# Four edits to the first stages of an attention and two-MLP kernel: where the decay factors are loaded, which banks the first transposes use, where the second group is normalised, and how far the second products lag

## The chip, the cores and the metric

The kernel runs on one core of one Trainium2 chip, as one program in one launch. The metric is the device time of one execution in microseconds; the median of several runs counts.

## The reference

The reference chains three computations. The first is a linear recurrence with a complex decay, for 4 batches, 8 heads, 768 steps and head size 48:

```python
scale = np.minimum(mag, 0.999) / (mag + 1e-06)         # mag = |a_re + i a_im|
for t in range(S):
    S_re, S_im = ar*S_re - ai*S_im + kv, ar*S_im + ai*S_re   # kv: outer product of k and v
    y[:, :, t] = einsum('bhd,bhde->bhe', q[:, :, t], S_re)
```

Its output, as 3072 tokens of 384 columns, goes through `silu(x @ w_gate) * (x @ w_val) @ w_out` with 1536 inner columns, and that through `h = x @ w_in; (h - tanh(h)) @ w2_out` with 2048 inner columns. The MLP weights are float64 arrays, all else is float32.

## The kernel before, in words

**Units and groups.** The recurrence is computed in 24 units of 128 steps (6 for each batch). Two units make a group. For each group, `group_steps` normalises the decays (`squares`, `norm_root`, `norm`), transposes them on PE (`put_a`: three transposes into one PSUM bank, then copies by ACT into the tile PL), forms running products of the complex decays in 14 dependent steps on DVE (`cstep`, L278 to L281), copies them into NW, works out a few small per-group factors (`lam`) and a reciprocal (W[2], L357 to L365). The factors are stored to DRAM (L351) and read back in another layout as the tile LS (L355, four loads of 3 KB). The first group is normalised before its transposes; the second inside the first group's `cstep` loop (L316 to L321); later ones inside the loop of the group ahead of them (L304).

For each unit, `unit_a` transposes q and k, scales them into QK (L390), stores QK to DRAM (L392) and reads it back as TK and TQ (L397). `unit_b` multiplies TK by TQ into scores (psS, L434), masks them, updates the running state (Hn, from Z and LS, on POOL, L427 to L429) and forms the output y, which goes by DMA into x, the input of the first MLP.

**MLP tiles.** `moe1_tile` runs the first MLP over 8 tiles of 2, 2, 2, 3, 3, 4, 4 and 4 units. Each has 12 steps f: 18 matmuls of the first layer (L581), silu on ACT (L585), a product and a split into a high and a low half (t, hi, lo; L590, L540, L541), and 9 matmuls of the second layer (L565), which wait in a list, `pend`, and are issued by `catch_up(lag)`. The lag is one step. Attention work for the next tile is traced between the matmuls (`bg`), and in the first tile also the decoding of the float64 weights (`dec1`, `decode`): DMA of the raw words, ACT L144, DVE L145 to L148, ACT L154, and then either two PE passes and ACT L164 or DVE L156. The weight of the second layer has two buffers (wo).

**Order.** Each engine runs its own list in order. The lists are drawn up when the program is built: a scheduler of the framework simulates time, and each engine takes, among the instructions whose inputs and buffers are ready at that simulated moment, the one that was traced first. `issue_after` holds a set of instructions behind a named one: the weights of the first tile (L719) are decoded after the last `cstep` of the first group. All DMAs are issued from one queue, SP's.

**PSUM.** There are eight banks: two named at, one psA (used by `put_a`), two l1 and three l2. Until the first MLP tile begins, `PA` hands out the two at and three l2 banks in turn (L130).

Of the kernel before, what the change touches and what calls it, by code (L numbers as in the profile page):

```python
# [8 lines left out]
F32 = mybir.dt.float32  # L9
F32R = mybir.dt.float32r  # L10
# [7 lines left out]
P = 128  # L18
# [23 lines left out]
def tile_kernel(ctx: ExitStack, tc: tile.TileContext, q, k, v, a_re, a_im, w_gate, w_val, w_out, w2_in, w2_out, out):  # L42
# [18 lines left out]

    N_PRE, QAT, QDEP = 8, 15, 4
    SHARE0, SHARE1, SHARE, RATE = 1, 0, 2.0, 6
    NORM_AT, NA0, SCM = 5, 1, 8

    N_A, N0, W2STEP, LON = 8, 20, 2, 10
    TU = max(TILES)
# [195 lines left out]

    def put_a(u, g, pl, PL, A0):
        t = st["a"][pl][:, g]
        ps = ps_g.tile([P, 512], F32, tag="psA", name="psA")
        for j in range(NJ):
            PE.transpose(ps[:, P * j:P * (j + 1)], t[:, P * j:P * (j + 1)], ident)
        p = ps[:, 0:DM].rearrange("p (j t) -> p j t", j=NJ)
        for h, x in ((1, p[:, :, HALF:P]), (0, p[:, :, HALF:0:-1])):  # L270
            ACT.copy(out=PL[:, :, pl, :, g, :, h].rearrange("p e b j -> p j b e"), in_=x.rearrange("p j (b e) -> p j b e", e=8))
        ACT.copy(out=A0[:, pl, :, g], in_=p[:, :, 0])
# [10 lines left out]
    def group_steps(g0):  # L283
        grp = list(range(g0, g0 + G))

        PL = pl_p.tile([P, 8, 2, 8, G, NJ, 2], F32, tag="PL", name="PL")
        A0 = a1.tile([P, 2, NJ, G], F32, tag="A0", name="A0")
        if g0 == 0:
            squares(DVE)
            norm_root(0)  # L290
            norm(DVE)
            yield
        for g, u in enumerate(grp):
            for pl in (1, 0):
                put_a(u, g, pl, PL, A0)
                yield
        load_a(g0 + G)
        for c in range(2):
            DVE.memset(PL[:, 0, c, 0, :, :, 0], 1.0 - c)
        flat = PL.rearrange("p e c b g j h -> p e c (b g j h)")  # L300
        for e in range(1, 8):
            cstep(flat[:, e - 1], flat[:, e], 1)
            yield
            if e == NORM_AT and 0 < g0 < NU - G:  # L304
                squares(POOL)
                norm_root(g0 + G)
                yield
                norm(POOL)
                yield
        rows = PL.rearrange("p e c b g j h -> p (e c) b (g j h)")  # L310
        for b in range(1, 8):
            cs = cstep(rows[:, 14:16, b - 1], rows[:, :, b], 8)
            if g0 == 0:
                prog["cs"] = cs.ins
            yield
            if g0 == 0 and b == NA0:  # L316
                squares(DVE)
                norm_root(G)
                yield
                norm(DVE)  # L320
                yield  # L321

        NW = a1.tile([P, 3, G, NJ, P], F32, tag="NW", name="NW", bufs=1)
        for c in range(2):
            nw = NW[:, c].rearrange("p g j (h b e) -> p h (g j) b e", h=2, e=8)
            ACT.copy(out=nw[:, 1], in_=PL[:, :, c, :, :, :, 1].rearrange("p e b g j -> p (g j) b e"))
            ACT.copy(out=nw[:, 0], in_=PL[:, ::-1, c, ::-1, :, :, 0].rearrange("p e b g j -> p (g j) b e"))
        yield

        sh = [P, 2, NJ, G]  # L330
        T0, pr = T("T0", sh), T("lp", [P, 2, 2, NJ, G])
        for i in range(2):
            DVE.tensor_tensor(out=pr[:, i], in0=PL[:, 7, :, 7, :, :, 0].rearrange("p c g j -> p c j g"), in1=A0[:, i].unsqueeze(1).to_broadcast(sh), op=ALU.mult)
        DVE.tensor_tensor(out=T0[:, 0], in0=pr[:, 0, 0], in1=pr[:, 1, 1], op=ALU.subtract)
        DVE.tensor_tensor(out=T0[:, 1], in0=pr[:, 1, 0], in1=pr[:, 0, 1], op=ALU.add)
        WL = a2.tile([P, 2, NJ, G + 1], F32, tag="wl", name="WL")
        DVE.tensor_copy(out=WL[:, :, :, 1:G + 1], in_=PL[:, 7, :, 7, :, :, 1].rearrange("p c g j -> p c j g"))
        if g0 > 0:
            DVE.tensor_copy(out=WL[:, :, :, 0], in_=st["wl"][:, :, :, G])
        else:  # L340
            DVE.memset(WL[:, :, :, 0], 1.0)
        st["wl"] = WL
        pr2 = T("lp", [P, 2, 2, NJ, G])
        for i in range(2):
            DVE.tensor_tensor(out=pr2[:, i], in0=T0, in1=WL[:, i, :, 0:G].unsqueeze(1).to_broadcast(sh), op=ALU.mult)
        L = a1.tile([P, NJ, 3, G], F32, tag="lam", name="lam")
        DVE.tensor_tensor(out=L[:, :, 0, :], in0=pr2[:, 0, 0], in1=pr2[:, 1, 1], op=ALU.add)
        DVE.tensor_tensor(out=L[:, :, 1, :], in0=pr2[:, 1, 0], in1=pr2[:, 0, 1], op=ALU.subtract)
        DVE.tensor_tensor(out=L[:, :, 2, :], in0=pr2[:, 0, 1], in1=pr2[:, 1, 0], op=ALU.subtract)
        lam_g = lam_d[g0 // G]  # L350
        SP.dma_start(out=lam_g.rearrange("(j p) c g -> p j c g", p=P), in_=L)  # L351
        LS = a2.tile([D2, H, 2, G], F32, tag="ls", name="LS")
        for i in range(2):
            for c in range(2):
                SP.dma_start(out=LS[i * D:(i + 1) * D, :, c, :], in_=lam_g[:, c * (1 + i), :].rearrange("(h d) g -> d h g", h=H))  # L355
        yield
        W = [NW[:, c].rearrange("p g j t -> p (g j t)") for c in range(3)]  # L357
        x1, x2 = W[2], T("x2")
        ACT.activation(out=x1, in_=W[0], func=AF.Square)
        ACT.activation(out=x2, in_=W[1], func=AF.Square)  # L360
        DVE.scalar_tensor_tensor(out=x1, in0=x1, scalar=-1.0, in1=x2, op0=ALU.mult, op1=ALU.subtract)
        ACT.activation(out=x2, in_=x1, func=AF.Abs_reciprocal_sqrt, scale=-1.0, bias=tiny)
        ACT.activation(out=x2, in_=x2, func=AF.Square, accum_out=chk[:, 1, g0 // G:g0 // G + 1])
        DVE.tensor_tensor(out=x1, in0=x1, in1=x2, op=ALU.mult)
        DVE.scalar_tensor_tensor(out=W[2], in0=x1, scalar=2.0, in1=x2, op0=ALU.add, op1=ALU.mult)  # L365
        yield
        for g, u in enumerate(grp):
            st["w", u] = (NW, LS, g)
        yield

    def unit_a(u):


        qn, kn = st.pop(("q", u)), st.pop(("k", u))
        NW, LS, g = st["w", u]
        W = [NW[:, c, g] for c in range(3)]
        qk = a1.tile([P, 2, NJ, P], F32, tag="qk", name="qk")
        for i, x in enumerate((qn, kn)):
# [16 lines left out]
        for i, x in ((1, TK), (0, TQ)):  # L395
            for c in range(2):
                SP.dma_start(out=x[c * D:(c + 1) * D], in_=d[i, c].rearrange("(h d) t -> d h t", h=H))  # L397
        yield
        Kn = a1.tile([P, H, 2, D], F32, tag="Kn", name="Kn")
        for c in range(2):  # L400
# [142 lines left out]
    def MT(tag, bufs, dt=F32):  # L543
        return m1.tile([P, N1], dt, tag=tag, name=tag, bufs=bufs)
# [7 lines left out]
    def moe1_tile(ti, bg):  # L552
# [3 lines left out]
        tok = tile_u0[ti] * P  # L556
        acc = []

        def l2(f, m):
            if f == 0:  # L560
                acc.extend(ps_2.tile([P, 512], F32, tag="l2", name="acc")[:, 0:n_t] for _ in range(NJ))
            w = wo_t.pop(ti * NF1 + f)
            for j in range(NJ):
                for i, (a, b) in enumerate(PASSES):
                    PE.matmul(acc[j], lhsT=w[:, a, j * P:(j + 1) * P], rhs=m[b], start=(f == 0 and i == 0), stop=(f == NF1 - 1 and i == 2))  # L565
            if f == NF1 - 1:

                oh, ol = (t[:, :, 0:n_t] for t in x)
                for j in range(NJ):
                    ACT.copy(out=oh[:, j], in_=acc[j])  # L570
                    DVE.tensor_tensor(out=ol[:, j], in0=acc[j], in1=oh[:, j].bitcast(F32), op=ALU.subtract)  # L571
                for c, t in enumerate((oh, ol)):
                    SP.dma_start(out=o_d[:, c, :, tok:tok + n_t], in_=t.bitcast(F32))

        for f in range(NF1):
            ps = []
            for i, w in enumerate((wg_hl[f], wv_hl[f])):
                p = ps_1.tile([P, 512], F32, tag="l1", name="l1")[:, 0:n_t]
                for n in range(3 * NJ):
                    kk, (a, b) = n // 3, PASSES[n % 3]  # L580
                    PE.matmul(p, lhsT=w[a][:, kk], rhs=x[b][:, kk, 0:n_t], start=(n == 0), stop=(n == 3 * NJ - 1))  # L581
                ps.append(p)
                if i == 0:
                    s = MT("t", MID)[:, 0:n_t]
                    ACT.activation(out=s, in_=p, func=AF.Silu)  # L585
                    if f == 0:
                        catch_up(0)
                    bg(2 * f)
            catch_up(1)
            DVE.tensor_tensor(out=s, in0=s, in1=ps[1], op=ALU.mult)  # L590
            m = [MT(tag, MID, F32R)[:, 0:n_t] for tag in ("hi", "lo")]
            split(s, *m)
            load_wo(ti * NF1 + f)
            pend.append(lambda f=f, m=m: l2(f, m))
# [336 lines left out]
```

## Time and profile before

| what | value |
|---|---|
| median of 3 runs | 1236.8 us (1231.5 to 1237.46) |
| profiled execution, its own time | 1240.99 us |
| its span | 1239.2 us |
| PE, PEld, DVE, ACT busy | 1092.8, 972.8, 987.2, 655.7 us |
| mean granted TensorE clock | 0.943 of full speed |

The profile comes from one execution. Busy times of different engines overlap. Times of PE are modelled and overlap one another in dense stretches. The first matmul of the first MLP starts at 118.36 us, the second tile begins at about 200.5 us and the third at about 276 us.

### The profile page before, as it was taken

The numbers are of one execution on the slowest core, as the hardware profiler recorded it, in microseconds if no ns is written. First come the engines' busy times: TensorE is split into PE (matmuls) and PEld (weight loads), VectorE is DVE, ScalarE is ACT, GpSimd is POOL, SyncE is SP. The second block draws the span as 40 slices with busy tenths as digits, with TensorE's granted clock in tenths as the row PEclk, the third lists the DMA queues.
The fourth block names the chain that finished last, engine by engine and source line by source line (L and its number), as shares of the span: only waits on it lengthen the run. The fifth ranks groups of instructions, "written<-read, shape, count | busy, mean of one in ns | idle before, by whom it ended". The sixth has DMA issues, their size and how long they took to land. (4 is left out here: it accounts for less than half of the span.)

```text
span 1239.2 us, 18491 instructions
## 1 busy us (share of the span) xinstructions
PE 1092.8 (88%) x6504; PEld 972.8 (78%) x6504; DVE 987.2 (80%) x2010; ACT 655.7 (53%) x1247; POOL 125.9 (10%) x110
## 2 busy tenths in 40 slices
PE   3157857879989999889999999989999999999997
PEld 2145846878988888877878888878999999999996
DVE  4878968965979788596885338989888888888886
ACT  5446537375563754536535224565565655555553
POOL 0012321202122122021211000000000000000000
PEclk9567977998999999889999999999999999999999
DMA  6397777887886878686666658642100102020000
GB/s 152 74 214 173 159 162 191 218 187 189 207 206 145 198 195 184 146 216 151 151 165 170 169 138 282 211 158 95 51 27 25 53 1 77 1 77 1 26 1 28
DMA packets 296741, 163.37 MB, mean 132 GB/s; under 512 B 157505, under 2 KB 273857, under 8 KB 296641
## 3 DMA queue, kind: packets, MB, share of 16 engines
q1 hardware_dynamic: 296640, 162.11, 52.1%
q8 instruction: 53, 0.87, 0.3%
q14 instruction: 48, 0.39, 0.1%
HBM read 111.82 MB, written 37.86 MB: 121 GB/s over the span
## 5 line engine op out<-in xcount | busy, mean ns | idle before, releaser
L581 PE MATMUL l<-x,wgv 128*128 128x256 f32 (+2 forms) x1728 | 351.9, 351 | 12.7 <-ACT t L585 10.3
L581 PEld LDWEIGHTS l<-x,wgv 128*128 128x128 f32 x1728 | 285.6, 197 | 42.4 <-ACT t L585 13.8
L663 PE MATMUL l<-x,wi 128*128 128x512 f32 x864 | 214.0, 393 | 5.0 <-DVE t L611 5.0
L645 PE MATMUL l<-w,hi 128*128 128x384 f32 x768 | 190.2, 338 | 0.0
L663 PEld LDWEIGHTS l<-x,wi 128*128 128x128 f32 x864 | 161.1, 188 | 34.8 <-DVE t L611 6.1
L565 PE MATMUL acc<-hi,wo 128*128 128x256 f32 (+2 forms) x576 | 166.9, 350 | 8.5 <-ACT wo L154 3.4
L540 ACT CAST hi<-t 128x512 fp32r<-128x512 f32 (+2 forms) x192 | 108.6, 566 | 120.8 <-DVE t L590 89.6
L645 PEld LDWEIGHTS l<-w,hi 128*128 128x128 f32 x768 | 140.9, 189 | 7.8 <-DVE x L571 0.4
L541 DVE TENSOR_TENSOR lo<-t,hi 128x512 fp32r<-128x512 f32 (+2 forms) x192 | 124.6, 649 | 27.1 <-ACT hi L540 26.8
L604 ACT ACTIVATE t<-l 128x512 f32<-128x512 f32 x96 | 57.3, 597 | 147.1 <-PE l L663 143.0
L645 PE MATMUL l<-w,lo 128*128 128x384 f32 x384 | 122.3, 337 | 0.4 <-DVE lo L541 0.4
L565 PEld LDWEIGHTS acc<-hi,wo 128*128 128x128 f32 x576 | 105.6, 195 | 19.6 <-ACT wo L154 4.2
L278 DVE TENSOR_TENSOR prod<-PL 128x384 f32<-128x384 f32 x168 | 105.3, 627 | 2.7
L565 PE MATMUL acc<-lo,wo 128*128 128x256 f32 (+2 forms) x288 | 98.2, 345 | 0.0
L434 PE MATMUL psS<-TQ,TK 96*128 96x128 f32 x384 | 61.1, 314 | 38.1 <-DMA TQ<-qk_d 21.7
L606 DVE TENSOR_TENSOR l<-l,t 128x512 f32<-128x512 f32 x96 | 67.0, 698 | 33.5 <-ACT uu L605 33.3
L434 PEld LDWEIGHTS psS<-TQ,TK 96*128 96x128 f32 x384 | 56.8, 223 | 43.2 <-issue 24.7
L590 DVE TENSOR_TENSOR t<-t,l 128x256 f32<-128x256 f32 (+2 forms) x96 | 52.5, 547 | 33.6 <-PE l L581 20.1
L611 DVE COPY_PREDICATED t<-far,l 128x512 f32<-128x512 int32 x96 | 71.0, 739 | 2.6
L585 ACT ACTIVATE t<-l 128x256 f32<-128x256 f32 (+2 forms) x96 | 47.1, 490 | 48.3 <-PE l L581 44.2
L645 PEld LDWEIGHTS l<-w,lo 128*128 128x128 f32 x384 | 71.4, 188 | 0.8 <-DVE lo L541 0.8
L610 DVE SCALAR_TENSOR_TENSOR t<-vv,t 128x512 f32<-128x512 f32 x96 | 66.1, 689 | 6.8
(128 smaller groups left out, 1670.6 us busy)
## 6 DMA issues: line engine op xcount, KB each, us to landing
wo<-wo_d SPq DMA_DIRECT2D x84, 384.0 KB, 4.0
qk_d<-QK SPq DMA_DIRECT2D x24, 768.0 KB, 5.0
TK<-qk_d SPq DMA_DIRECT2D x48, 192.0 KB, 4.2
TQ<-qk_d SPq DMA_DIRECT2D x48, 192.0 KB, 4.9
x<-o_d SPq DMA_DIRECT2D x12, 768.0 KB, 6.0
x<-y SPq DMA_DIRECT2D x48, 144.0 KB, 4.4
raw<-in_moe_w_in_dram SPq DMA_DIRECT2D x16, 384.0 KB, 4.1
raw<-in_moe_w_out_dram SPq DMA_DIRECT2D x16, 384.0 KB, 3.2
```

Source lines behind the costliest of these rows:

```text
L278: DVE.tensor_tensor(out=pr, in0=prev.unsqueeze(2).to_broadcast(sh), in1=cur.unsqueeze(1).to_broadcast(sh), op=ALU.mult)
L434: PE.matmul(ps[:, P * i:P * (i + 1)], lhsT=TK[:, 4 * hh + i], rhs=TQ[:, 4 * hh + i], start=True, stop=True)
L540: ACT.copy(out=hi, in_=t)
L541: DVE.tensor_tensor(out=lo, in0=t, in1=hi.bitcast(F32), op=ALU.subtract)
L565: PE.matmul(acc[j], lhsT=w[:, a, j * P:(j + 1) * P], rhs=m[b], start=(f == 0 and i == 0), stop=(f == NF1 - 1 and i == 2))
L581: PE.matmul(p, lhsT=w[a][:, kk], rhs=x[b][:, kk, 0:n_t], start=(n == 0), stop=(n == 3 * NJ - 1))
L604: ACT.activation(out=t, in_=p, func=AF.Tanh)
L606: DVE.tensor_tensor(out=p, in0=p, in1=t, op=ALU.subtract)
L610: DVE.scalar_tensor_tensor(out=t, in0=vv, scalar=G_F, in1=t, op0=ALU.add, op1=ALU.mult)
L611: DVE.copy_predicated(out=t, mask=far, data=p)
L645: PE.matmul(acc[tb], lhsT=g[a][:, tb * P:(tb + 1) * P], rhs=w2_hl[f][:, b], start=(f == 0 and n == 0), stop=(f == NF2 - 1 and n == 2))
L663: PE.matmul(p, lhsT=wi_hl[a][:, kk, sl], rhs=x[b][:, kk, :], start=(n == 0), stop=(n == 3 * NJ - 1))
```

## The change

Four edits. (1) LS is no longer loaded in `group_steps` behind the store of the factors, but in `unit_a` of the first unit of a group, behind the loads of TK and TQ. (2) `put_a` of the first two units takes its bank from `PA` instead of the single bank psA. (3) The three calls that normalise the second group move from the eighth `cstep` of the first group to the end of its `group_steps`. (4) In MLP tiles 0 and 1, `catch_up` leaves four steps waiting instead of one, the list is not emptied at the start of tile 1, and t, hi and lo of two steps share one buffer of 512 columns (each step of these tiles has 256).

```diff
     def put_a(u, g, pl, PL, A0):
-        ps = ps_g.tile([P, 512], F32, tag="psA", name="psA")
+        ps = PA("psA") if u < 2 else ps_g.tile([P, 512], F32, tag="psA", name="psA")
...
-            if g0 == 0 and b == NA0:
-                squares(DVE)
-                norm_root(G)
-                yield
-                norm(DVE)
-                yield
...
-        LS = a2.tile([D2, H, 2, G], F32, tag="ls", name="LS")
-        for i in range(2):
-            for c in range(2):
-                SP.dma_start(out=LS[i * D:(i + 1) * D, :, c, :], in_=lam_g[:, c * (1 + i), :].rearrange("(h d) g -> d h g", h=H))
...
-            st["w", u] = (NW, LS, g)
+            st["w", u] = [NW, None, g]
         yield
+        if g0 == 0:
+            squares(DVE)
+            norm_root(G)
+            yield
+            norm(DVE)
+            yield
...
         for i, x in ((1, TK), (0, TQ)):
             for c in range(2):
                 SP.dma_start(out=x[c * D:(c + 1) * D], in_=d[i, c].rearrange("(h d) t -> d h t", h=H))
+        if g == 0:
+            LS = a2.tile([D2, H, 2, G], F32, tag="ls", name="LS")
+            for i in range(2):
+                for c in range(2):
+                    SP.dma_start(out=LS[i * D:(i + 1) * D, :, c, :], in_=lam_d[u // G][:, c * (1 + i), :].rearrange("(h d) g -> d h g", h=H))
+            for n in range(G):
+                st["w", u + n][1] = LS
...
+        near = ti < 2
...
-                    s = MT("t", MID)[:, 0:n_t]
+                    if not near:
+                        s = MT("t", MID)[:, 0:n_t]
+                    else:
+                        if f % 2 == 0:
+                            mid = [MT(tag, MID, dt) for tag, dt in (("t", F32), ("hi", F32R), ("lo", F32R))]
+                        s, *m = [t[:, f % 2 * (N1 // 2):][:, 0:n_t] for t in mid]
                     ACT.activation(out=s, in_=p, func=AF.Silu)
-                    if f == 0:
+                    if f == 0 and ti != 1:
                         catch_up(0)
                     bg(2 * f)
-            catch_up(1)
+            catch_up(4 if near else 1)
             DVE.tensor_tensor(out=s, in0=s, in1=ps[1], op=ALU.mult)
-            m = [MT(tag, MID, F32R)[:, 0:n_t] for tag in ("hi", "lo")]
+            if not near:
+                m = [MT(tag, MID, F32R)[:, 0:n_t] for tag in ("hi", "lo")]
```

## Rows read from the trace of the kernel before

**Rows 1.** Windows by stage: span, busy time of each engine, granted clock, DMA share, GB/s.
```profile
0.00:118.36 118.36, 52.74 (x230) 35.11 (x230) 88.82 (x195) 61.76 (x121) 13.48 (x23) 0.74 0.66 148
118.36:200.50 82.14, 58.45 (x437) 54.56 (x438) 67.43 (x145) 44.76 (x92) 22.82 (x15) 0.81 0.73 166
200.50:276.00 75.50, 62.90 (x510) 58.90 (x508) 62.29 (x153) 45.55 (x93) 12.31 (x10) 0.95 0.83 207
276.00:420.00 144.00, 129.43 (x998) 125.64 (x999) 111.15 (x257) 79.19 (x159) 29.42 (x24) 0.94 0.78 184
420.00:1239.20 819.20, 789.30 (x4334) 698.57 (x4332) 657.54 (x1264) 424.45 (x784) 47.83 (x38) 0.98 0.41 110
```
**Rows 2.** PE's waits, first two MLP tiles: waiter, ender, us in total, times, longest.
```profile
PE psA L268 <- ACT A L272: 14.3, 4, 11.7
PE l L581 <- ACT t L585: 6.7, 6, 2.0
PE psS L434 <- DMA TQ<-qk_d: 6.1, 3, 5.1
PE acc L565 <- ACT wo L154: 3.4, 3, 1.9
PE acc L565 <- DMA wo<-wo_d: 1.9, 3, 0.9
PE acc L565 <- DVE wo L156: 1.1, 2, 0.5
PE acc L565 <- ACT hi L540: 0.9, 1, 0.9
```
**Rows 3.** Timeline of ACT around the first transposes: start, duration, instruction, idle before.
```profile
25.68 0.84 ACT L271 COPY PL<-psA 128x192 f32<-128x192 f32 x2 [1.64 <-PE psA L268]
...
26.36 0.89 ACT L164 CAST wgv<-psL 128x384 fp32r<-128x384 f32 x2
...
32.22 0.21 ACT L272 COPY A<-psA 128x3 f32<-128x3 f32 x1
```
**Rows 4.** Timeline of DVE during the first group's steps.
```profile
32.58 0.56 DVE L278 TENSOR_TENSOR prod<-PL 128x384 f32<-128x384 f32 x1
...
33.64 0.56 DVE L278 TENSOR_TENSOR prod<-PL 128x384 f32<-128x384 f32 x1
...
38.79 0.95 DVE L241 TENSOR_TENSOR s<-s,s 128x768 f32<-128x768 f32 x1
...
52.76 1.02 DVE L145 TENSOR_SCALAR dt<-dt 128x768 f32<-128x768 f32 x2
53.70 0.24 DVE L333 TENSOR_TENSOR lp<-PL,A 128x12 f32<-128x12 f32 x2
```
**Rows 5.** Timeline of SP's queue around the first load of LS.
```profile
65.92 4.82 SPq L355 DMA_DIRECT2D LS<-lam_d  x4
...
71.98 0.41 SPq L392 DMA_DIRECT2D qk_d<-QK  x1
```
**Rows 6.** Timeline of DVE: the first unit's QK.
```profile
66.00 1.82 DVE L390 TENSOR_TENSOR QK<-qk,NW 128x768 f32<-128x768 f32 x2
```
**Rows 7.** PE's waits before the first MLP tile.
```profile
PE psS L434 <- DMA TQ<-qk_d: 6.9, 1, 6.9
```
**Rows 8.** DMA issues of the whole span: count, KB each, median us to landing.
```profile
TQ<-qk_d SPq DMA_DIRECT2D x48, 192.0 KB, 4.9
...
LS<-lam_d SPq DMA_DIRECT2D x48, 3.0 KB, 2.5
```
**Rows 9.** Timeline of ACT shortly before the first MLP tile.
```profile
108.60 0.87 ACT L326 COPY NW<-PL 128x384 f32<-128x384 f32 x1 [0.83 <-DVE PL L280]
109.37 0.58 ACT L468 CAST y<-psY 128x512 fp32r<-128x512 f32 x1
```
**Rows 10.** Timeline of PE in the first MLP tile.
```profile
187.16 0.90 PE L268 MATMUL psA<-ident,ar 128*128 128x128 f32 x3 [11.70 <-ACT A L272]
```
**Rows 11.** Window of 20 us around it, columns as in the first group.
```profile
180.00:200.00 20.00, 9.75 (x41) 8.66 (x42) 15.80 (x41) 16.87 (x35) 3.35 (x3) 0.50 0.62 147
```

More of the change, by code (lines that the diff above doesn't have):

```diff
@@ L63, in tile_kernel @@
     SHARE0, SHARE1, SHARE, RATE = 1, 0, 2.0, 6
-    NORM_AT, NA0, SCM = 5, 1, 8
+    NORM_AT, SCM = 5, 8
     N_A, N0, W2STEP, LON = 8, 20, 2, 10
@@ L367, in group_steps @@
         for g, u in enumerate(grp):
-            st["w", u] = (NW, LS, g)
+            st["w", u] = [NW, None, g]
         yield
+        if g0 == 0:
[4 more added lines that the diff above has]
+            yield
     def unit_a(u):
         qn, kn = st.pop(("q", u)), st.pop(("k", u))
-        NW, LS, g = st["w", u]
+        NW, _, g = st["w", u]
         W = [NW[:, c, g] for c in range(3)]
```

## The prediction

> **What bounds the kernel now.** I read the stages first, then what PE waits for in each, then the timelines around the four edits. The chain that ended last names only the last store and says nothing of the start. The stages [rows 1] show two kernels in one. From 276 us on PE is busy 129.4 of 144.0 and 789.3 of 819.2 us: PE's own work sets the time there, and nothing in the change touches that work. Before 118.36 us the first MLP has not begun, and PE has only decoding and attention to do. Between 118.36 and 276 us, in the first two MLP tiles, PE stands still for 82.14 - 58.45 = 23.7 and 75.50 - 62.90 = 12.6 us, together 36.3, and runs the first tile at a mean clock of 0.81. DVE is the busiest of the others (67.4 of 82.1, 62.3 of 75.5), and DMA is at 0.73 and 0.83. So the change can be worth two things: the moment at which the first tile starts, and part of those 36.3 us. A start that comes earlier is kept to the end, if the stage after it can follow, because PE is full from 276 us on.
>
> **The change part by part.**
>
> **Banks.** In the kernel before the four sets of transposes of units 0 and 1 share one bank, so each waits until ACT has emptied it, and ACT meanwhile takes decoding casts. ACT begins the copies at 25.68 and ends the last at 32.22 + 0.21 = 32.43 [rows 3], 6.75 us for four sets. One set holds ACT for 26.36 - 25.68 = 0.68 us, the start of its first copy to the start of what follows; four back to back take 2.7, end at about 28.5, and save 3.9. The other bound is 0, if a cast still falls between every two sets. I take 3.0: the first cast pair (0.89 us [rows 3]) still gets in once. The decoding is pushed back by as much; its cover is that the weights are first used at 118.36 us, and if that cover is gone the 3.0 go with it. Giving PA four more turns changes which bank a later tile gets, not how many there are: 0, and at most the 0.9 of one such set of transposes [rows 10] either way.
>
> **Norm of the second group.** The 14 steps run from 32.58 to 52.76, 20.2 us. Undisturbed a step takes 33.64 - 32.58 = 1.06, 14 take 14.8: the second group's norm costs the first group 5.4 us [rows 4]. Behind the group it would give 5.4 back. But the edit changes only the order of tracing, and the scheduler fills by readiness. Decoding traced far later stands right behind the last step (52.76), ahead of the group's own product L333 (53.70) [rows 4], since L333's input was not ready; and the norm's first sum runs at 38.79, behind the sixth step (32.58 + 6 x 1.06 = 38.9), though it was traced behind the eighth. As the steps depend on one another, each leaves a gap, and the norm is ready in the same gaps as before. So I take 0. Bounds: a gain of 5.4, and a loss of 5.4, if what the first group gains the second loses and the second ends last [rows 9].
>
> **LS.** The four loads hold SP's queue from 65.92 to 70.74, because the factors' store has to land first. The first unit's QK is ready at 66.00 + 1.82 = 67.82 and its store leaves at 71.98 [rows 5, 6]: 4.2 us late. Behind that store hang TK, TQ and the scores, for which PE then waits 6.9 us [rows 7]; the second unit follows on the same buffers. Moved, the loads pass an ar load, weight loads, the store and TK and TQ. I take 3.9 of the 4.2, since the ar and weight loads still stand in the queue; bounds 0 (queue held by something else) and 4.8 (all of the hold). In exchange four issues of about 0.4 us, as the store's [rows 5], now stand between TQ and the weight loads behind it: 1.6 us, covered because decoding runs ahead of its use. LS itself lands 1.6 + 2.5 = 4.1 us after TQ's issue, TQ 4.9 [rows 8], so no unit waits for it: 0. If it did, the price would be 1.6 for each of the two groups that follow in tiles 0 and 1, 3.2 together.
>
> Does the start keep 3.0 + 3.9 = 6.9? The last link before 118.36 is y of the second unit, which stands on ACT behind a copy that waits for the second group's steps on DVE [rows 9]. DVE is busy 88.8 of 118.4 us [rows 1], so it has 29.5 idle from which to make up 6.9, and the same two edits start its work earlier. I keep all of it; the lower bound is 0.
>
> **Lag.** With four steps waiting, a second product no longer stands close behind its split, its weight or its cast. What PE waited for at the products themselves is 3.4 + 1.9 + 1.1 + 0.9 = 7.3 us [rows 2], and this goes. Three things come late next. The weight has two buffers, so the weight of step f + 2 can be finished only once product f is done; product f + 2 is two steps later, as before. A buffer of hi and lo holds two steps, so in every even step ACT's cast waits for a product issued in that same step: 12 such steps; ACT is busy 44.8 of 82.1 and 45.6 of 75.5 us [rows 1] and covers it, but queued behind that cast on ACT are the silu of the next step, which frees the l1 bank for PE, and the copies that free psA. And tile 1's first product comes one step, not two, behind tile 0's last, whose three banks have to be emptied in between. For these I set 2.8 against the 7.3, an estimate by L581's own longest wait (2.0) and the one cast wait (0.9) [rows 2]. Net 4.5. Bounds: 7.3 + 6.7 = 14.0, if the waits for silu go too, and -6.7, if these double.
>
> What lies behind an engine's front can't come forward: the transposes at 187.16 waited 11.7 us [rows 10], and second products stood right behind them. The Trainium skill (PSUM — Partial Sum Buffer, Engine vs sequencer instructions) says that matmuls start and complete in program order. By that rule a product that is ready four steps early is worth only the 7.3 us of its own waits; without it, it could reach into all 36.3. The trace agrees: no matmul ran in those 11.7 us.
>
> Sum: 3.0 + 0 + 3.9 + 4.5 = 11.4 us. Within the profiled execution: 1240.99 (span 1239.2, 1.8 around it) becomes 1229.6. That execution lies 4.2 above the median of the runs, 1236.8, and I predict against the median: 1236.8 - 11.4 = 1225.4, so 1225.
>
> **The rivals.**
>
> A: the norm truly stands behind the first group, because buffers or ACT hold it back. Then 5.4 more come off the start: 1220. For it: 5.4 us stand in the rows as the norm's. Against it: the early sum and the decoding in the gaps [rows 4].
>
> B: the start is earlier, but the first two tiles give it back, and the lag only moves waits. For it: 14.3 + 6.7 + 6.1 = 27.1 us of waits there [rows 2] (psA, silu, TQ) are not removed by any edit, and DVE is at 82% in both tiles [rows 1], with the same decoding and attention to do. Against: DVE has 28 us idle there. Then 6.9 and 4.5 are both lost: 1237.
>
> C, slower: one more set of later transposes falls into the wrong place. From unit 2 on psA is still a single bank, emptied by ACT in its order, and PE's order is fixed when the program is built; every edit redraws it. One such wait cost 11.7 us [rows 10], and around it the clock was 0.50, the lower of the two levels (1.2 GHz), at which 9.75 us of PE's work [rows 11] take about 4.9 longer than at the upper: 16.6 in all. With four products behind it, it takes the lag's gain too: 1236.8 - 6.9 + 16.6 = 1246.5. It decides as soon as the new order has one more wait of over 7 us at L268 than the old. For it: psA is the largest wait of the stage [rows 2]. Against: there were four of them, only one of them long, and the redrawn order may as well lose that one.
>
> **How the numbers follow.** Forecast 0.49 (its own range 1215 to 1231), A 0.14, B 0.20, C 0.17. The range: below, A with the lag's upper bound, 1219 - 9.5 = 1210; above, C's middle part up to 1244, leaving out about one in ten on each side. Within 0.5% is 1230.6 to 1243.0, about what a measurement of this kernel can tell from no change. Faster: 0.45 of the forecast's 0.49, A's 0.14 and 0.03 of B: 0.62. Slower: 0.14 of C and 0.03 of B: 0.17. Same: the rest, 0.21.
>
> **What would show it.** Banks: the first step on DVE near 29.6 instead of 32.58. Norm: its sums still between the first group's steps, which last about 20 us; 15 would be A. LS: the store of QK within 1 us of QK's end, at about 66; the first matmul of the first MLP near 111.5. Lag: no wait of PE at L565 in the first two tiles, and the third tile beginning near 264 to 265. Wrong would be a first tile that starts at 111 and a third that still begins near 276 (B), an L268 wait of over 7 us more (C), or waits at L581 for silu well over 6.7 us.

## The result and the profile after

The changed kernel takes 1245.2 us (median of 5, 1242.66 to 1247.34) against 1236.3 us for the kernel before on the same chip (median of 5, 1231.5 to 1237.46): ratio 1.0072, interval 1.0057 to 1.0087. It is slower by about 9 us where 11 us of gain were forecast, and lies just above the forecast's range (1210 to 1244).

The two profiled executions differ by less: 1242.66 us is the fastest of the kernel after, and 1240.99 us lies above all five timed runs of the kernel before. So the traces tell where work went, and the ratios tell how much.

The stages of the kernel after, columns as in [rows 1]; the first ends where the first MLP tile begins:

```profile
0.00:104.11 104.11, 43.55 (x221) 28.39 (x221) 73.11 (x149) 54.19 (x105) 9.72 (x22) 0.80 0.74 162
104.11:200.00 95.89, 68.13 (x431) 61.62 (x432) 80.33 (x183) 45.81 (x93) 14.83 (x13) 0.77 0.61 159
200.00:280.00 80.00, 65.88 (x549) 62.34 (x548) 65.90 (x165) 53.03 (x109) 16.69 (x14) 0.92 0.81 191
280.00:420.00 140.00, 122.43 (x937) 116.49 (x936) 107.66 (x249) 76.79 (x154) 27.88 (x24) 0.94 0.76 177
420.00:1241.00 821.00, 795.05 (x4373) 704.23 (x4372) 657.77 (x1267) 427.42 (x788) 44.81 (x38) 0.99 0.41 111
```

The first tile begins 14.3 us earlier than before (104.11 against 118.36). Only 65.62 - 60.56 = 5.06 us of that are idle time of PE that is gone; the other 9.2 are work that PE has not done yet (43.55 us busy ahead of the tile, 52.74 before [rows 1]). Up to 200 us PE then stands still for 95.89 - 68.13 = 27.8 us, against 82.14 - 58.45 = 23.7 in a shorter stretch before [rows 1].

A tile has 216 matmuls of the first layer, so the start of each tile can be counted. In the kernel before the second tile begins at 205.07 and the third at 281.82; the 200.5 and 276 of the section on its profile are the ends of the first layers ahead of them. In the kernel after the first tile's end at 154.87, the second tile begins at 211.78, 6.7 us later than before, and the third at 276.95, 4.9 us earlier. PE's lines at the three starts, and those of the kernel before at the last two:

```profile
104.11 1.19 PE L587 MATMUL l<-x,wgv 128*128 128x256 f32 x4 [7.39 <-DMA x<-y]
...
211.78 1.31 PE L587 MATMUL l<-x,wgv 128*128 128x256 f32 x6
...
276.95 4.18 PE L587 MATMUL l<-x,wgv 128*128 128x256 f32 x18 [4.84 <-DMA x<-y]
```

```profile
205.07 1.33 PE L581 MATMUL l<-x,wgv 128*128 128x256 f32 x9 [1.43 <-ACT t L585]
...
281.82 2.27 PE L581 MATMUL l<-x,wgv 128*128 128x256 f32 x9
```

The waits at 104.11 and 276.95 are for x, the output of the attention. Such a wait is by itself no mark of a slow kernel: e1 and e5 below, both faster than the kernel before, wait 5.4 and 5.9 us for x where their second tile begins, at 193.5 and 194.6. What sets the kernel after apart (and e2 below, from 164.9 to 208.9) is a stretch without any matmul of the first layer. Counted for L587 alone (length, PE, PEld, clock, DMA share, GB/s), there is none from 156 to 211 us,

```profile
156.00:211.00 55.00, 0.00 (x0) 0.00 (x0) 0.74 0.72 183
```

until the last piece of unit 3's x has come, 28 us later than before (first the kernel after, then the kernel before):

```profile
207.17 2.73 SPq L492 DMA_DIRECT2D x<-y  x4
```

```profile
179.07 2.52 SPq L488 DMA_DIRECT2D x<-y  x4
```

PE fills part of that stretch with second products and attention. Its waits from 104 to 277 us, columns as in [rows 2], where no wait for x stands:

```profile
PE l L587 <- DMA x<-y: 12.2, 2, 7.4
PE psS L438 <- DMA TQ<-qk_d: 9.9, 3, 4.3
PE psA L268 <- ACT A L272: 7.5, 3, 4.3
PE acc L571 <- ACT wo L154: 5.8, 4, 2.5
PE l L587 <- ACT t L597: 5.0, 7, 2.2
PE psK L407 <- DVE QK L386: 4.9, 1, 4.9
PE acc L571 <- DVE wo L156: 1.5, 2, 0.8
PE acc L571 <- DMA wo<-wo_d: 0.8, 1, 0.8
```

So the attention of units 2 and 3, the second group, is late. DVE shows by how much: the first group's steps start at 29.31 and run undisturbed to 44.0, those of the second start at 94.82 (65.5 before):

```profile
29.31 0.56 DVE L278 TENSOR_TENSOR prod<-PL 128x384 f32<-128x384 f32 x1
...
43.01 0.56 DVE L278 TENSOR_TENSOR prod<-PL 128x384 f32<-128x384 f32 x1
...
53.46 0.96 DVE L355 SCALAR_TENSOR_TENSOR NW<-NW,x 128x768 f32<-128x768 f32 x1
...
60.25 1.82 DVE L386 TENSOR_TENSOR QK<-qk,NW 128x768 f32<-128x768 f32 x2
...
62.85 0.95 DVE L256 TENSOR_TENSOR s<-s,s 128x768 f32<-128x768 f32 x1
...
73.41 0.95 DVE L262 TENSOR_TENSOR ar<-ar,s 128x768 f32<-128x768 f32 x1
...
94.82 0.56 DVE L278 TENSOR_TENSOR prod<-PL 128x384 f32<-128x384 f32 x1
```

Between them stands the second group's norm, now 48 to 74 us (its last part, L256 to L262, on DVE). On ACT its squares (L239) stand right behind L350, which writes x2, a temporary of the first group's reciprocal, and the root (L247) stands behind that reciprocal's last use of x2 (L355 above) and a weight's DMA:

```profile
47.76 0.83 ACT L350 ACTIVATE x<-NW 128x768 f32<-128x768 f32 x1
48.49 0.83 ACT L239 ACTIVATE s<-ar 128x768 f32<-128x768 f32 x1
...
57.26 0.89 ACT L144 ACTIVATE dt<-x 128x768 f32<-128x768 f32 x1 [2.93 <-DMA x<-in_moe_w_val_dram]
...
58.41 0.95 ACT L247 ACTIVATE y<-s,tiny 128x768 f32<-128x768 f32 x1
```

SP's queue has the second group's factors at 140.47 and the third unit's QK at 160.86 (118.36 and 126.01 before). The loads of LS still leave ahead of the first unit's QK, as in [rows 5], but hold the queue for 1.85 us and not 4.82, and QK is ready only at 60.25 + 1.82 = 62.07, when they are through:

```profile
57.04 1.85 SPq L399 DMA_DIRECT2D LS<-lam_d  x4
58.94 0.47 SPq L190 DMA_DIRECT2D x<-in_moe_w_val_dram  x1
59.45 0.46 SPq L191 DMA_DIRECT2D x<-in_moe_w_val_dram  x1
62.10 0.38 SPq L388 DMA_DIRECT2D qk_d<-QK  x1
```

The lateness does not simply run on to the end. The factors of the second and third group are stored 22 and 26 us later than before, those of the fifth, at 298.3, are 6.4 us ahead, and those of the sixth are 3.2 behind (356.45 against 353.27). The fourth MLP tile begins at 361.9 (354.6 before), and by 420 us PE has stood still for 120.0 us, against 116.5 before. These traces do not show by which chain of waits the late second group becomes the 9 us of the medians.

### The profile page after: what moved, and what is told of

It reads as the page before. It is cut to its first block, busy times and chain, and to the rows that moved or that the text cites. A ratio compares the mean times of both kernels' runs of the same rounds, so it can differ in the third digit from the quotient of the medians.

```text
span 1241.0 us, 18479 instructions
## 1 busy us (share of the span) xinstructions
PE 1095.0 (88%) x6504; PEld 973.1 (78%) x6504; DVE 984.8 (79%) x2010; ACT 657.2 (53%) x1247; POOL 113.9 (9%) x110
## 5 line engine op out<-in xcount | busy, mean ns | idle before, releaser
L587 PE MATMUL l<-x,wgv 128*128 128x256 f32 (+2 forms) x1728 | 353.9, 352 | 25.0 <-DMA x<-y 12.2
L587 PEld LDWEIGHTS l<-x,wgv 128*128 128x128 f32 x1728 | 286.5, 198 | 55.4 <-ACT t L597 15.3
L571 PEld LDWEIGHTS acc<-hi,wo 128*128 128x128 f32 x576 | 104.9, 193 | 23.7 <-ACT wo L154 6.8
L278 DVE TENSOR_TENSOR prod<-PL 128x384 f32<-128x384 f32 x168 | 98.6, 587 | 3.1
L438 PE MATMUL psS<-TQ,TK 96*128 96x128 f32 x384 | 60.8, 312 | 24.7 <-DMA TQ<-qk_d 18.4
```

Source lines behind the costliest of these rows:

```text
L278: DVE.tensor_tensor(out=pr, in0=prev.unsqueeze(2).to_broadcast(sh), in1=cur.unsqueeze(1).to_broadcast(sh), op=ALU.mult)
L438: PE.matmul(ps[:, P * i:P * (i + 1)], lhsT=TK[:, 4 * hh + i], rhs=TQ[:, 4 * hh + i], start=True, stop=True)
```

## The experiments

All were timed against the kernel before on the same chip. The table has the ratio with its interval, and from each profiled execution the span, the first matmul of the first MLP and the stores of the factors of groups 1, 2, 3 and 6 (us from the span's start).

| kernel | ratio | span | first tile | group 1 | 2 | 3 | 6 |
|---|---|---|---|---|---|---|---|
| before | 1 | 1239.2 | 118.4 | 62.0 | 118.4 | 184.3 | 353.3 |
| after | 1.0072 (1.0057 to 1.0087) | 1241.0 | 104.1 | 51.9 | 140.5 | 210.0 | 356.4 |
| e1, after without the norm's move | 0.9968 (0.9950 to 0.9985) | 1234.4 | 116.7 | 62.4 | 118.6 | 195.2 | 353.1 |
| e2, norm alone | 1.0083 (1.0053 to 1.0112) | 1244.8 | 110.0 | 54.3 | 144.1 | 209.3 | 362.8 |
| e3, lag alone | 0.9968 (0.9948 to 0.9988) | 1235.3 | 118.3 | 61.6 | 118.7 | 182.1 | 350.1 |
| e4, LS and banks | 1.0056 (1.0036 to 1.0076) | 1248.5 | 116.1 | 61.6 | 118.5 | 193.3 | 366.1 |
| e5, after, x2 with its own buffer | 0.9973 (0.9955 to 0.9992) | 1232.8 | 116.7 | 62.0 | 119.2 | 196.2 | 351.1 |
| e6, banks alone | 1.0064 (1.0039 to 1.0088) | 1243.2 | 115.5 | 61.2 | 118.0 | 193.2 | 363.2 |
| e7, LS alone | 0.9995 (0.9979 to 1.0011) | 1231.9 | 117.8 | 61.7 | 117.7 | 182.1 | 348.3 |
| e8, LS forced behind TQ | 1.0047 (1.0022 to 1.0071) | 1247.2 | 121.1 | 61.8 | 118.9 | 191.1 | 365.0 |
| e9, after, PA for units 2 and 3 too | 1.0038 (1.0017 to 1.0059) | 1236.3 | 121.9 | 51.9 | 126.2 | 197.9 | 353.5 |
| e10, before with more PE work in tile 0 | 1.0017 (0.9996 to 1.0037) | 1232.7 | 117.2 | 60.8 | 117.0 | 187.2 | 347.9 |
| e11, lag and LS | 1.0024 (1.0005 to 1.0043) | 1236.1 | 117.0 | 60.5 | 117.2 | 183.7 | 347.3 |
| e12, e5 without the banks | 1.0025 (1.0004 to 1.0045) | 1237.0 | 117.9 | 61.9 | 117.9 | 183.0 | 350.2 |
| e13, norm moved, x2 with its own buffer | 0.9988 (0.9972 to 1.0004) | 1233.7 | 117.1 | 61.3 | 116.7 | 181.4 | 347.9 |
| n2, half copies swapped | 1.0028 (1.0011 to 1.0046) | 1239.8 | 117.6 | 61.3 | 117.6 | 187.7 | 359.1 |
| n4, first column first | 1.0049 (1.0027 to 1.0072) | 1238.7 | 120.3 | 62.0 | 115.4 | 191.2 | 354.4 |
| n5, planes swapped | 1.0028 (1.0009 to 1.0048) | 1236.8 | 117.8 | 61.0 | 117.8 | 192.1 | 352.8 |

### Which edit: e1 to e4

e1 is the change with the norm's calls back behind the eighth `cstep`; e2 the kernel before with only the norm moved; e3 with only the lag; e4 with LS and banks.

```diff
+            if g0 == 0 and b == NA0:
+                squares(DVE)
+                norm_root(G)
+                yield
+                norm(DVE)
+                yield
...
-        if g0 == 0:
-            squares(DVE)
-            norm_root(G)
-            yield
-            norm(DVE)
-            yield
```

> The changed kernel with only the second group's norm put back to the eighth step of the first group; banks, LS and lag as changed. Theory 1 (the norm behind the first group makes the second group late, its factors are stored at 140 instead of 118 us, and tile 1 waits for units 2 and 3): faster than before, 1224 to 1231, the second group's factors stored before 115 and the second tile begun before 197. Theory 2 (the lag of four steps costs the time): still 1241 to 1248. Theory 3 (the LS loads or the banks redraw the order for the worse): still above 1240.

> The kernel before with only the second group's norm moved behind the first group. Theory 1: slower, 1243 to 1255, with the second group's factors stored at 135 us or later. Theory 2 and theory 3: within 4 us of before.

> The kernel before with only the lag of four steps and the shared buffers in the first two tiles. Theory 1: 1229 to 1238, no wait at the second products. Theory 2: slower, 1242 to 1250, with longer waits for silu or at the casts of hi. Theory 3: within 4 us of before.

> The kernel before with only the LS loads behind TK and TQ and the first transposes in five banks. Theory 1: 1227 to 1233, first MLP matmul at 110 to 114 us. Theory 2: the same, 1227 to 1233. Theory 3: slower than before by 4 us or more.

The norm's move carries the loss: without it the change is 0.3% faster than the kernel before (e1), alone it costs 0.8% (e2). e1's gain is smaller than expected, 4 us, and its second group's store at 118.6 is not the one before 115 that was expected. e2 has the same picture as the kernel after, group 1 eight microseconds earlier and group 2 26 us later. The lag gains 0.3% (e3), and the waits at the second products are gone but for 2.7 us, against 7.3 before [rows 2]. In the same stretch, though, PE's waits for TQ rise from 6.1 to 13.9 us and those at psA fall from 14.3 to 6.3, each by more than that gain. From e3's PE waits, 118 to 276 us:

```profile
PE psS L434 <- DMA TQ<-qk_d: 13.9, 4, 6.9
PE psA L268 <- ACT A L272: 6.3, 4, 2.4
...
PE acc L567 <- ACT hi L540: 1.2, 1, 1.2
PE acc L567 <- ACT wo L154: 1.0, 2, 0.5
...
PE acc L567 <- DVE wo L156: 0.5, 1, 0.5
```

e4 missed: LS and banks were expected to gain, and lose 0.6%.

### Why the norm came late: e5, e13, e9

`T` hands out three buffers of one tag ("gt"), and s1, s2, y0 and x2 all come from it. In the kernel before the norm's temporaries are traced ahead of x2, in the change behind it. e5 gives the first group's x2 its own buffer, and e13 puts that and the moved norm alone into the kernel before:

```diff
-        x1, x2 = W[2], T("x2")
+        x1, x2 = W[2], T("x2") if g0 else T("x20", [P, G * DM])
```

> The changed kernel with one difference: the first group's temporary x2 gets a buffer of its own, and no longer takes one of the three that the second group's norm needs. Theory 1a (the norm is held back by the order in which those three buffers are given out, not by its place in the trace): the norm's first square runs near 32 us, between the first group's steps, the second group's factors are stored before 122, and the time is that of the kernel with the norm put back, 1230 to 1240. Theory 1b (the place in the trace holds it back): the square stays behind 45 us and the time at 1243 to 1250.

> The kernel before with the second group's norm traced behind the first group, as in the change, and the first group's x2 in a buffer of its own. Buffer theory (the norm was late only because its three temporaries are handed out in the order of tracing, behind x2): the second group's factors are stored at about 118 to 120 us, as before, and the time is within 0.5% of before, against 1.008 for the moved norm without the buffer. Rival (the place in the trace itself holds it back): the store is at about 140 us again and the ratio near 1.008.

In e13 the calls still stand behind the whole group in the code, and yet the norm runs among the first group's steps. ACT's first square waits for nothing but its input, and runs 12 us earlier than in the kernel after:

```profile
36.48 0.84 ACT L239 ACTIVATE s<-ar 128x768 f32<-128x768 f32 x1 [3.39 <-DMA ar<-in_a_re_dram]
```

The second group's store is back at 119.2 and 116.7, and the loss is gone (0.9973 and 0.9988). This separates two things that e2 had together. The place of the calls costs nothing that can be measured (0.9972 to 1.0004); three shared buffers for which x2 is traced ahead of the norm cost 1.0083 - 0.9988 = 0.95% here, some 12 us, and 1.0072 - 0.9973 = 0.99% in the change. Both are about twice the largest effect of a redrawn order below (0.49%).

The norm ends at 74.4 in the kernel after, but the second group's steps begin 20 us later still. In between are four sets of transposes at 78.66, 83.16, 87.94 and 91.89 through the one bank psA. e9 takes their bank from PA too:

```diff
-        ps = PA("psA") if u < 2 else ps_g.tile([P, 512], F32, tag="psA", name="psA")
+        ps = PA("psA") if u < 4 else ps_g.tile([P, 512], F32, tag="psA", name="psA")
```

> The changed kernel, with the transposes of the first four units instead of two in the five banks. Theory 1 with the single bank as a part (the second group's transposes, each waiting for ACT to empty psA, add to its lateness): its factors are stored 5 to 15 us earlier than 140 and the time falls by 2 to 8 us, 1237 to 1243. Theory 1 without it (the norm's own delay is all): the store stays at 138 or later and the time within 3 us of the changed kernel, 1242 to 1248.

The second store comes 14 us earlier (126.2) and about half of the loss goes (1.0038 against 1.0072; their intervals just touch), while the first tile begins 18 us later, at 121.9. The second tile begins earlier, at 195.71 against 211.78. A kernel whose first tile starts far later is, by these medians, the faster one.

### Is the start worth anything: e10

e10 is the kernel before with the first-layer matmuls of the first four steps of tile 0 done twice, 72 matmuls more.

```diff
-                for n in range(3 * NJ):
+                for n in (2 if ti == 0 and f < 4 else 1) * list(range(3 * NJ)):
```

> The kernel before with the first layer's matmuls of the first four steps of tile 0 done twice: 72 more matmuls, 8 to 9 us of PE's time at the pace of the rows (0.12 each), with the same output. Theory P (as predicted: the start and pace of the first MLP tile carry through to the end): 5 to 9 us slower, 1241 to 1246. Theory S (the supply of attention units sets when the tiles after the first can go on, and PE has room in tile 0): within 3 us of before.

From its first tile's start to 200 us PE is busy 70.1 of 82.8 us instead of 58.5 of 82.1 [rows 1], at a granted clock of 0.96 instead of 0.81, and the time changes by 2 us (interval of the ratio 0.9996 to 1.0037):

```profile
117.17:200.00 82.83, 70.12 (x579) 66.96 (x580) 72.15 (x158) 48.11 (x99) 20.15 (x15) 0.96 0.76 185
```

The edit redrew the order too. PE's waits at psA, 14.3 us before [rows 2], are 2.6 here from 117 to 277 us:

```profile
PE psA L268 <- ACT A L272: 2.6, 3, 1.0
```

The first tile's first layer ends at 184.73 with its 72 matmuls more, 16 us earlier than before (200.67), and the second tile begins at 187.01 (205.07 before). So e10 sets no price on the 72 matmuls. What it shows is that this lead is not kept: the third tile begins at 277.73, 4.1 us earlier than before, and the time is no lower.

Over the 18 kernels of the table the span hardly goes with the start of the first tile (correlation -0.23) and closely with the store of the sixth group's factors (0.94; 0.75 us of span for each us of that store). Both are read from the same single executions; with the measured ratios in place of the spans, the correlations are -0.40 and 0.68. That the attention's pace sets the time is what this suggests; no run shows it.

### LS: e7, e8, e11

> The kernel before with only the LS loads traced behind TK and TQ. Theory A (the edit doesn't do what it says: the scheduler puts the loads where their input is ready, ahead of the store of QK): the loads still hold the queue by about 5 us from 66 to 71, the store of QK leaves near 72, and the time is within 5 us of before. Theory B (the loads stand behind the queries): the store leaves near 68 and the time is 2 to 4 us lower.

> The kernel before with the LS loads forced behind the last load of TQ by an order edge on the queue, so that the edit does what it says. The price of the hold (3.9 of 4.2 us, as predicted): the store of QK leaves near 68, the first MLP matmul near 114, and the time is 1231 to 1237. The rival (the queue is held by something else, or the rest of the first two tiles gives it back): within 3 us of before or slower.

e7 is the edit alone, e8 the same with the loads held behind TQ:

```diff
-                SP.dma_start(out=x[c * D:(c + 1) * D], in_=d[i, c].rearrange("(h d) t -> d h t", h=H))
+                tq = SP.dma_start(out=x[c * D:(c + 1) * D], in_=d[i, c].rearrange("(h d) t -> d h t", h=H))
...
+                  with tc.issue_after(tq.ins):
...
```

In e7 the loads, although traced behind TQ, leave ahead of the store of QK as before:

```profile
66.02 4.10 SPq L399 DMA_DIRECT2D LS<-lam_d  x4
...
71.36 0.41 SPq L388 DMA_DIRECT2D qk_d<-QK  x1
```

The edit does nothing there, and the time is that of the kernel before (0.9995). In e8 they do leave behind TQ, and the store of QK is hardly earlier (71.23 against 71.98): another DMA, a weight load, now holds the queue in their place for about as long.

```profile
66.07 4.56 SPq L190 DMA_DIRECT2D x<-in_moe_w_val_dram  x1
...
71.23 0.38 SPq L388 DMA_DIRECT2D qk_d<-QK  x1
...
77.30 0.99 SPq L393 DMA_DIRECT2D TQ<-qk_d  x2
78.72 3.44 SPq L400 DMA_DIRECT2D LS<-lam_d  x4
```

The expected 4 us were not there to be had. Added to the lag (e11), the edit that did nothing by itself gives 1.0024 where the lag alone has 0.9968:

> The kernel before with the lag of four steps and the LS loads traced behind TK and TQ; no banks, norm as before. If the gains of the lag alone (4 us) stand and LS is worth nothing: 1230 to 1236, faster than before by 0.2 to 0.5%. If each edit mainly redraws the order: anything from 1228 to 1245.

### The banks, and what a redrawn order is worth: e6, e12, n2, n4, n5

> The kernel before with only the first transposes in five banks. Theory A (the order of the later stages is redrawn and costs): first step near 30 us instead of 32.6, but the time 4 us or more above before, as with banks and LS together. Theory B (banks are free): within 3 us of before or faster.

> The changed kernel with a buffer of its own for x2 and the first transposes back in the single bank: lag, LS and the moved norm remain. If banks cost what they cost alone (8 us) and the norm is harmless once it isn't held back: 1226 to 1233, faster than both. If the banks cost nothing beside the lag: as the kernel with x2's own buffer, 1230 to 1236.

e6 has only the edit to `put_a`. The first step comes at 30.21 (32.58 before), and the first group's store at 61.2 (62.0): the norm, still among the steps, takes most of it back. The second group is no later either (118.0). Then something else is: on ACT the second group's root for W[2] (L362) stands behind a decoding step that waits for a DMA, and starts at 119.38, against 115.50 before; the third store comes at 193.2 against 184.3.

```profile
115.41 0.84 ACT L360 ACTIVATE x<-NW 128x768 f32<-128x768 f32 x1
...
118.93 0.55 ACT L144 ACTIVATE dt<-x 128x384 f32<-128x384 f32 x1 [1.94 <-DMA x<-in_moe_w_out_dram]
119.38 0.92 ACT L362 ACTIVATE x<-NW,tiny 128x768 f32<-128x768 f32 x1
```

These 3.9 us are a place in an order, nothing that banks cost; where the other 5 us of the third store come from is not shown. If the banks cost their 0.6% anywhere, e12, the change without the banks and with x2 apart, should have been the best. It is 0.25% slower than the kernel before, and e5, the same with the banks, 0.27% faster. To see how much an order is worth by itself, three edits change no work at all: in `put_a`, the two half copies in the other order (n2), the copy of the first column ahead of them (n4), the real plane ahead of the imaginary one (n5). The edits of n2 and n5:

```diff
-        for h, x in ((1, p[:, :, HALF:P]), (0, p[:, :, HALF:0:-1])):
+        for h, x in ((0, p[:, :, HALF:0:-1]), (1, p[:, :, HALF:P])):
...
-            for pl in (1, 0):
+            for pl in (0, 1):
```

> The kernel before, with the two half copies that empty psA in put_a issued in the other order: the same instructions, the same buffers, only the order in which the program is written down. Theory R (each edit redraws the lists of the whole program, and a redrawn list is by itself worth 0.3 to 0.6%): the ratio to the kernel before lies anywhere from 0.994 to 1.006, and the three such edits of this set spread by 0.4% or more; then the +0.6% of the banks alone and the +0.2% of lag with LS are no price of those edits. Rival O (the sizes belong to the edits themselves): all three within 0.2% of before, 1234 to 1239.

> The kernel before, with put_a's copy of the first column into A0 issued ahead of its two half copies instead of behind them. Theory R: a ratio anywhere from 0.994 to 1.006; a spread of 0.4% or more over the three. Rival O: within 0.2% of before.

> The kernel before, with put_a called for the real plane ahead of the imaginary one. Theory R: a ratio anywhere from 0.994 to 1.006; a spread of 0.4% or more over the three. Rival O: within 0.2% of before.

They cost 0.28%, 0.49% and 0.28%. They do not spread by the 0.4% expected (0.21%), and all three medians lie off the kernel before by more than the 0.2% that the rival allowed, though only n4's interval leaves that out (the lower ends are 0.1, 0.3 and 0.1%). So an edit that does no more than redraw the order can cost 3 to 6 us. The +0.6% of the banks and the +0.5% of e8 are little more than that, so no price of their own has been shown for either.

## Why the prediction was wrong

**Norm: the step that failed.** "As the steps depend on one another, each leaves a gap, and the norm is ready in the same gaps as before. So I take 0." The inputs were ready; the buffers, for which x2 stood ahead, were not (e5 and e13). The text on the order of the kernel before says that an engine takes instructions "whose inputs and buffers are ready"; the working looked at the inputs alone. Rival A named buffers and ACT as what could hold the norm back, and its mark (14 steps in about 15 us) came true: 29.31 to 44.0. But its sign was wrong. The bound beside it, "a loss of 5.4, if what the first group gains the second loses and the second ends last", had the right outcome and a price by the wrong row: 5.4 us is what the norm takes of DVE, while the second group lost 29 us at its first step (94.82 against 65.5). The norm's move costs 0.83% alone (e2), about 10 us; within the change, 1.0072 - 0.9968 = 1.04%, about 13 us.

**"A start that comes earlier is kept to the end".** This held neither in the kernel after (first tile 14 us earlier, 9 us slower) nor in e10 (second tile 18 us earlier, no faster). The condition set in the prediction, "if the stage after it can follow", was the question itself: the stage after needs units 2 and 3, and PE's 23.7 idle us in the first tile [rows 1] were a sign that it waits for them already. Rival B put this at 0.20, and e1, where the start is 1.6 us earlier and the third store 11 us later, is nearer to it than to the forecast. The sign "a third that still begins near 276" can't be read as it was meant: by the count above the third tile of the kernel before begins at 281.82, and 276 is the end of the first layer ahead of it.

**Banks: 3.0 at the first step.** Right in place, 32.58 - 29.31 = 3.3 in the kernel after, but no gain by the end follows from it: alone the banks lose 0.6% (e6), and the change with x2 apart is 0.5% faster with them than without (e5 against e12). The prediction looked for a cover of the decoding pushed back, and did not ask what the first group's earlier end redraws behind it.

**LS: 3.9 of the 4.2.** The lower bound, "0 (queue held by something else)", is what e7 and e8 show. The edit does not move the loads past the store (e7), and where they are moved a weight load of 4.56 us stands in the gap (e8). The order in which DMAs are traced is not that of the queue: the scheduler put the loads as soon as their source was stored. The prediction applied that rule to the norm and not to the loads. In the kernel after its sign came true all the same, the store within 1 us of QK's end (62.10 and 62.07), but by luck: the loads were through early, and QK itself came later behind them.

**Lag: 7.3 - 2.8 = 4.5.** Alone it gives 0.32%, 4 us (e3), the one term of the right size, with 4.6 of the 7.3 us of waits gone. That may be luck: other waits of the same stretch moved by 8 us each, and with LS, an edit worth nothing alone, the lag is 0.24% slower than the kernel before (e11). The Trainium skill (PSUM — Partial Sum Buffer, Engine vs sequencer instructions) has matmuls start and complete in program order; e3 agrees so far that the gain stayed within the products' own waits. In the kernel after the waits at the second products are 8.1 us, and 5.8 of them are for the weight itself (wo, on ACT), which a lag of the products does not bring forward.

**Rival C** is not what happened, though its 1246.5 lies next to the measured 1245.2: the waits at L268 fell from 14.3 to 7.5 us, none over 4.3, so that closeness is luck. But its ground, that every edit redraws the order, was the sounder part of the prediction.

**The sum.** Single terms measured alone give -0.3 (lag) - 0.05 (LS) + 0.6 (banks) + 0.8 (norm) = +1.1% against the measured 0.7%, and without the norm +0.3% against e1's -0.3%. The first difference is within what the intervals of the four terms allow, the second is not: the terms do not simply add. The lower end of the range was worked out from 1219 where rival A gives 1220; nothing hangs on it. What stays open is what the banks and the forced LS cost in an order that is not redrawn, which these kernels cannot show, by which chain the late second group reaches the end, and why the kernel before lies ahead of all three neighbours.

Three versions beat both kernels: e1 (0.9968), e5 (0.9973) and the lag alone (e3, 0.9968). By the neighbours' spread, a gain of 0.3% can be a lucky order as well as the lag.

## What to carry to other kernels

Before you call a moved step free because its inputs are ready, list the buffers that it takes from a shared tag and who is traced ahead of it for them. An early start is worth only what the stage behind it can use: look for what that stage waits for, and if it idles already, speed up its supplier. In a kernel whose order is drawn up by a scheduler, time two or three edits that change no work, before a few tenths of a per cent are read as the price of an edit.

## What was not expected of the hardware

In e10 more matmuls in the first tile went along with a higher clock: a mean of 0.96 between its two levels (1.2 and 2.4 GHz) from 117.17 to 200 us, with PE busy 70.1 of 82.8 us, against 0.81 with 58.5 of 82.1 [rows 1]. The stretches differ in more than the 72 matmuls, though: e10 has no wait at psA over 1.0 us, while the kernel before has one of 11.7 us [rows 10], with a clock of 0.50 around it [rows 11]. Some of the added work may have been paid for by the clock; no run here separates the two.
